# Block 1 of a fused linear-attention and GEGLU kernel: three of its tile pairs in Strassen form, and its order written out as a list

## Chip, cores, metric

The program runs on one core of a Trainium2 chip. The metric is the device time of one execution in microseconds (us), as the median of several runs; four runs of the kernel before were taken. One further execution was recorded by the hardware profiler; all durations of single instructions come from it.

## What is computed

The reference, cut to what matters (q, k, v are 8 x 8 x 576 x 64, so x is 4608 x 512; d_ff is 1536; all fp32):

```
q_s = softmax(q, axis=-1)                 # over the head dimension
k_s = softmax(k, axis=2)                  # over the sequence
kv  = einsum('bhsd,bhse->bhde', k_s, v)
x   = einsum('bhsd,bhde->bhse', q_s, kv)  # then heads side by side: 4608 x 512
g, val = x @ w_gate, x @ w_val
out = (gelu(g) * val) @ w_out             # exact gelu
```

## The kernel before

**Blocks.** The 4608 rows of x are done in nine blocks of 512: block b (0 to 7) holds 512 of the 576 tokens of batch b, and a ninth (number 8) holds the 64 tokens left over from each batch. The order is 0 to 6, 8, 7. While the feed-forward part of block b runs, the attention of batch b + 1 is prepared: exp of q and k on ACT (`exp`), row sums of q on DVE (`norm_sum`, `norm_pair`) and the multiplication on POOL (`norm_mul`), the cast of v (`cast_v`), a DMA that transposes q (`unit_td`, issued by SP), the k/v products (`unit_kv4`) and their scaling (`kv4_norm`), and the product that makes the next x (`unit_x4`, emptied by `x4_out`).

**The feed-forward part, plain.** In block 0 and block 1, d_ff is cut into 12 tiles of 128. A tile has a gate product and a value product, four matmuls of 512 columns each (`mm_gv`); ACT takes gelu of the gate, DVE multiplies it with the value into `ht` (`gate`). In block 1 the first three tiles are interleaved with the last steps of the attention of batch 1 (`ffn_first`), the other nine follow one after the other (`ffn_fi`).

**The feed-forward part, in pairs.** From block 2 on, tiles k and k + 3 (k in 0 to 2), and likewise k and k + 3 for k in 6 to 8, form a pair, and their products are made by Strassen's scheme in Winograd's form: seven products P1 to P7 of 4 matmuls with 256 columns each (`product_gv`), 28 in place of 32 such halves. It needs sums of the weights (made once, by `sum_wgv` and `sum_w1`) and sums of x (`sum_x`, into `xs`), and more steps on ACT and DVE. The output product is made in the same scheme (`product`) in block 1 and after; it needs sums of `ht` (`sum_h`) and of `w_out` (`sum_w`).

**Order.** The order in which the program is written is the order on each engine: the engines run their own queues in order, and wait for each other by semaphores. In blocks 0 and 1 it comes from loops and from a table of riders, `at(block, kind, index, ...)`: functions that are called behind a tile (`FI`) or an output step (`NS`). From block 2 on it is a list of words for each block, `PROG[b]`, which `play` carries out one after the other:

- `kPi`: product Pi of pair k. `kc`: ACT copies bank a of pair k to bank b. `ks5`, `ks2`: a scaled copy to SBUF on ACT, with `d` on DVE. `ka2`, `ka5`: DVE adds a bank to such a copy, into a buffer `cc`. `kg2`, `kg4`: gelu of 256 columns on ACT; `km2`, `km4`: their multiplication on DVE. `ku`: gelu of half of `cc` on ACT; `kU`: its multiplication on POOL, with `d` on DVE.
- `Oi:js`: product i of the output, of some j or all six. `y1`, `y2`, `y5`: copies of output banks; `b+`, `a+`, `c+`: additions into the output rows, `ye` the last copy. `sij`: sum i of `ht`. `wki`: sum i of the weights of pair k. `xi`: sum i of the next x.
- `lq`, `lk`, `lv`: loads of the next batch, by SP. `NA`, `NB`: row sums of q; `M0` to `M3`: their use, on POOL. `t`: the transposing DMA. `K`, `k`, `X`, `Xa`, `Xd`: k/v products, their scaling, the product for the next x, its emptying on ACT and DVE. `Vi`: casts of v. `Eq`, `Ek`: exp of q, k. `TE`, `TG`: a preload of ACT's table for exp or gelu.
- A last letter p, d or a names the engine (POOL, DVE, ACT); `>` and `<` take a word for the block after or before.

**Banks.** PSUM has eight banks. `big` takes the bank at the head of the list `ring`; `hold` keeps it until `let_go`. Two banks are set apart in `att_ring` for the attention until `one_ring` puts them on the list. A matmul that takes a bank waits for the last reader of the tile that was in it.

**Riders of block 1 that the change touches** (line numbers of the file before are in the printed functions): exp of k of batch 2 in two halves behind tiles 4 and 11, the casts of v of batch 2 on POOL behind tile 5, the transposing DMA behind tile 8, and

```
    at(1, NS, 2, L(unit_kv4, 2), L(exp, "k", 3), L(load_batch, 3, ((v, "v"),)), L(cast_v, 3, 0, H))
    at(1, NS, 4, L(unit_x4, 2, ("act", "dve"), 1), one_ring, L(preload, ACTF.Gelu))
```

Of the kernel before, what the change touches and what calls it, by code (L numbers as in the profile page):

```python
# [18 lines left out]
def kernel(  # L19
# [61 lines left out]
    def big(shape, dt, name, hold=False, seed=False):  # L81
        tag = ring.pop(next(i for i, x in enumerate(ring) if x in full) if seed else 0)
        t = ps_big.tile(shape, dt, name=name, tag=tag)
        words = 1
        for n in shape[1:]:
            words *= n
        (full.add if words == 512 and shape[0] == 128 and dt == f32 else full.discard)(tag)
        if hold:
            held[id(t)] = (t, tag)
        else:  # L90
            ring.append(tag)
        return t
# [434 lines left out]
    def ffn_first(xt, after):  # L527

        ps = []
        for fi in range(len(after)):  # L530
            psg = big([P, 512], f32, "psg")
            psv = big([P, 512], f32, "psv")
            if fi == 0:
# [6 lines left out]
            ps.append((psg, psv))  # L540
            for f in after[fi]:
                f()
        for fi, (psg, psv) in enumerate(ps):
            mm_gv(psg, wg_sb, xt, fi, [2])
            mm_gv(psv, wv_sb, xt, fi, [2])
        for fi, (psg, psv) in enumerate(ps):
            mm_gv(psg, wg_sb, xt, fi, [3])
            mm_gv(psv, wv_sb, xt, fi, [3])
            gate(psg, psv, fi)
# [110 lines left out]
    def product_gv(i, ps, xt, k, first):  # L660
        lo, hi = slice(k * P, (k + 1) * P), slice((k + NO // 2) * P, (k + NO // 2 + 1) * P)
        xs = xs_b[xt is st.get((B - 1, "xt"))]
        for t, w, nm in ((0, wv_sb, "v"), (1, wg_sb, "g")):
# [12 lines left out]
        2: ("lk lq lv 2P1 6P1 <x0d 0P1 <x2d 0P5 w71d 6P5 <x1d 6c w72d 6P2 0c w81d 6P6 0s5 0P6 6s5 0P3 6g2 w82p 6P3 "  # L676
            "0s2 NB 0P2 6m2 6s2 0P7 <x3p 0a2 6P7 0g2 1P5 2c 6a2 M3 1P1 0a5 2P2 0m2 2P5 w84p 1c 6a5 0P4 0u 1P2 2g2 6P4 "
            "M2 6u 1P6 0g4 NA 2P6 1s5 2m2 1P3 0U 0m4 1s2 7P1 1g2 2s5d 6g4 1P7 6U 2s2 1a2 2P3 6m4 2P7 7c 1m2 7P6 M0 "
            "1a5 8P1 7P2 2a2 1u 1P4 M1 8c 2a5 t 7P5 7g2 w83d 8P2 w74d 7s2 w73d 8P6 7s5 s01d 7P7 2u 8P5 1Ud 1g4 7P3 "
            "8s2 7a5 2P4 1m4 8s5 2U 8P7 7a2 8P3 2g4 7P4 >>lr s03p 7u 8a5 O1:03 O1:1 7g4 8a2 8P4 8g2 2m4 O1:4 7U 7m2 "  # L680
            "8u O1:25 8m2 8g4 K 7m4 8m4 O2 8U y1d TE s11d s21d s12d O5 s14d s02d s22d O6 Eq >lq b+ y5a k s24d X s04d "
            "s13d y2a O3:03142 s23d O7 Xa Xd V2a x2d x0d O3:5 x1d"),
        3: ("0P5 6P5 <a+ 0P1 <c+ 6P1 <Ek <O4 0s5 6c 0c NB 0P3 6s5 0P6 <yea 6P6 M3 6P3 0s2 NA 7P1 0P7 6s2d 6P2 6a2 <TG "
            "M0 6P7 0a2 0P2 6g2 1P1 0a5 7c <x3p 6m2 7P2 0g2 0P4 6a5 1c 6P4 0m2 M1 0u 1P6 0g4 1P5 7g2 7P5 7m2 6u 0U "
            "0m4 1P2 1s2 1P7 1s5d <V0p <V3a 7P6 6g4 6Ud 2P1 7s5 6m4 1P3 1g2 1a5 7P3 7s2 s01p 1P4 2c 1a2 7P7 1m2 8P1 "
            "1g4 M2 t 2P6 1u 7a5 2P5 <V1p 8c 1m4 7P4 2s2 7a2 8P5 2s5 1U 2P7 s02d 7u 8P6 7g4 O1:03 2a5 2P3 8s2 8P2 7Ud "
            "8s5 8P7 lk 2a2 O1:1 8P3 s11p 2u 2P2 8a5 8g2 8P4 7m4 8m2 2P4 2g2 2U O1:4 8g4 8a2 K 2g4 8m4 O2 2m4 8u s12p "
            "lv 2m2 8Ud s21d O1:25 TE s23d O5 s14d s04d y1a s22d O6 k b+ s24p y5d X Eq s03p O3:03142 Xa s13p Xd"),
        4: ("6P1 0P1 <y2d <x0d <O7 <Ek <x1p 0P5 0c NA <O3:5 0P6 6c <a+ <x3p 6P5 0s5 0P3 <c+ 0s2 6P2 <x2p 6s5 6P6 0P2 "
            "<V0a 6P3 M1 NB <O4 6s2d <TG 6g2 6a2 M0 0g2 1P1 0a2 <V2a 0P7 0m2 M3 6P7 1c 1P5 0a5 <V1a 1P6 6m2 M2 t 0P4 "  # L690
            "0u 6a5 7P1 <V3p <yea 1P2 0g4 1s5d 7P5 1s2 0Ud 6P4 1g2 0m4 1P3 7c 1m2 1P7 6u 2P1 6g4 1a2 7P6 7P2 7s5d lv "
            "6U 2c 7P3 1a5 7s2 2P5 6m4 7g2 7P7 s01p 7m2 2P6 2s5 7a2 1P4 s03p 1u 8P5 7a5 2s2 s02d 8P1 1g4 s04d 7P4 lq "
            "8s5 1m4 2P7 8c 1Ud 8P3 7u 8P6 7g4 2a5 2P3 2P2 7Ud 8s2 s11d 2P4 7m4 8P7 2g2 lk 8P2 8a2 s12p K 8a5 8g2 8P4 "
            "2g4 2a2 O1:03 8u 2m2 2m4 O1:1 8g4 O1:4 8m2 O1:25 2u 8m4 O2 8U k 2Ud TE s21d X y1a s22d O6 Xa Xd"),
        5: ("0P1 <s24d <x2d <O5 <x0d <s14d <s23d <s13d <Eq 0P5 lq 6P1 0c <b+ 0P2 <x1d <y5a 6P5 <Er <O3:03142 6c <x3p "
            "0s5 NB 0P6 6s5 6P6 <y2a <O3:5 6P3 M2 <O7 NA 6s2 0s2d 6P2 M0 Rr 6P7 6a2 0P7 <Ek M1 0P3 <a+ <O4 <c+ Rm <TG "
            "6a5 6g2 0g2 <V3p 6P4 6m2 0m2 1P1 <V1p <yea 1P5 6g4 0a2 7P5 6u 0a5 7P1 1c 0P4 0u 7s5d 1P2 6U 7c 1P6 1s5d "
            "6m4 7P6 <V2a 0g4 1P3 0U 1g2 1s2d 7P3 7s2 1P7 1a2 s01p 7P2 <V0a lv 2P1 7a2 2P5 1a5 M3 7P7 0m4 2c 1P4 1m2 "
            "7g2 s02d 8P1 1u 7m2 2P6 1g4 7a5 8P5 8c 7P4 t 1U 7u 2s2d 8P2 1m4 8s5 8P6 s03d 2s5 2P7 7g4 7Ud 8P3 s11d "
            "8s2 2P2 2a5 8P7 7m4 2P3 2g2 s12p 8g2 8a2 2P4 O1:03 8a5 lk s14p 8P4 8m2 2g4 O1:1 8u 2a2 O1:4 K 8g4 2m4 "  # L700
            "2m2 2u O1:25 8m4 8U O2 2Ud TE s21d s22d >tr y1a O5 s13d b+ s24d O6 s23d k Eq s04d X y5a O3:03142 y2d Xa "
            "O7 Xd x2d x0d"),
        6: ("6P1 <x1d <O3:5 <Ek 6P5 <a+ 0P1 6c <x3p 0P5 <V3a <O4 0c NA 6s5 <c+ 0s5 6P6 6P3 M1 <yea 0P6 <V0p 6P2 NB "
            "1P1 0P3 0s2d M0 0P2 6s2d 1c 0P7 6a2 6P7 M2 1P2 0a2 <TG 7P1 <V1p 6g2 0a5 1P6 0g2 6a5 0P4 0u 0m2 6P4 7c "
            "1g2 1P5 1s2d 0g4 7P6 6g4 0Ud 7P2 1m2 6u 0m4 1P7 1s5 6m4 7P5 7s2 2P1 6Ud 6m2 1P3 7s5 7P7 1a5 7g2 s01p 1P4 "
            "2c 1a2 2P5 7m2 7P3 1u 7a5 8P1 2s5 2P6 1g4 7a2 2P3 1U 8c 8P5 2s2d <V2a 8P6 2P2 7u 2a2 M3 t 1m4 2P7 8s2 "
            "7P4 2g2 7Ud 8P7 8s5 2a5 8P3 7g4 2P4 s11p 2u 8a5 O1:03 O1:1 2g4 8a2 8P2 7m4 2U 8P4 8u 2m2 2m4 K 8g2 8Ud "
            "O1:4 s21d O1:25 s23d O5 s12d s02d y1a s22d 8g4 8m2 O6 s04d 8m4 s03d s13d O2 s24d y2a k y5a O7 b+ s14d X "
            "O3:03142 a+ O4 Xa Xd"),
        8: ("0P1 <x0p <x2d <O3:5 6P1 <x1d 0P5 0c <c+ 6P5 6c 0P6 0s5 6P6 <yea 6s5d 6P2 z0d 0P3 z2d 7P1 6g2 0s2d 6P3 "  # L710
            "6s2 6m2 6P7 7c 0a2 0P7 1P1 6a2 7P2 0a5 7P6 1c 0P2 6a5 0u <x3d 7P5 6P4 0g2 0Ud 7g2 1P2 0m2 7s5 0P4 7s2d "
            "1P5 6u 7m2 6g4 1P6 1g2 6m4 0g4 7P3 7P7 1s5 6Ud 2P1 1s2 7a2 1P7 0m4 1P3 s01p 1m2 2c 2P5 7a5 2P6 z1p 2P2 "
            "1a5 7u 8P1 1a2 2s5 1P4 s02p 2s2d 2P3 8c 8P5 7Ud 2g2 8P6 2m2 1u 2P7 1g4 z3d 8P2 1Ud 8s2 7P4 8s5 2a5 8P7 "
            "8g2 1m4"),
# [459 lines left out]
```

The softmax here doesn't subtract the row's maximum and nothing guards it: scores larger than these inputs give would overflow.

## Time and profile before

| what | value |
|---|---|
| median of 4 runs | 288.78 us (288.70 to 288.96) |
| the profiled execution | 288.96 us, of which the span from first to last instruction is 287.2 us |
| busy share of the span | PE 97%, DVE 87%, ACT 73%, POOL 48% |
| granted TensorE clock | 1.00 of full speed over the span |
| HBM | 164 GB/s over the span |

The span is the time from the first to the last instruction on the core; 1.76 us lie around it. PE is TensorE's matmuls, PEld its weight loads, DVE VectorE, ACT ScalarE, POOL GpSimd, SP the engine that issues most DMAs. The busy time of PE contains matmuls that overlap, so single durations (273 ns for 256 columns) are longer than the distance from one start to the next. Where a row says "idle before", the engine stood still ahead of that instruction, and the name behind the arrow is what ended it.

In the recorded execution, block 1's first matmul starts at 48.72 us, its third tile's last at 55.14, its plain tiles end and its output begins at 70.89, and block 2's first product starts at 82.19.

### The profile page before, as it was taken

Reading aid. Unit: us, or ns where it says so; the run is one execution under the profiler, and the core shown is the slowest. Engines: PE = TensorE matmul, PEld = TensorE weight load, DVE = VectorE, ACT = ScalarE, POOL = GpSimd, SP = SyncE. Lnnn points to the kernel's source line nnn. Section 1 sums busy time; section 2 is a strip of 40 time slices with the busy share of each in tenths; the row PEclk is TensorE's granted clock in tenths of the full one; section 3 lists DMA queues with packets and bytes.
Section 4 is the critical chain, followed back from the end, with each engine's and each line's share of the span. In section 5 each row is a group of like instructions: output and inputs, shape, how many; then the busy total and the mean of one; then the engine's idle time right before and its main releaser. Section 6 shows DMA issues by size and latency. Waiting matters only on the chain.

```text
span 287.2 us, 6704 instructions
## 1 busy us (share of the span) xinstructions
PE 277.7 (97%) x2581; PEld 216.2 (75%) x2581; DVE 249.4 (87%) x497; ACT 209.9 (73%) x370; POOL 137.9 (48%) x128
## 2 busy tenths in 40 slices
PE   3999999999999999999999999999999999999994
PEld 1444445445888888888888888888888888888883
DVE  2854888877999999979989999999999799998993
ACT  3773367884798889978998899799794577716740
POOL 1567745988239731865864258542653104110110
PEclk9999999999999999999999999999999999999999
DMA  6999999999139916159149853690304030003303
GB/s 218 375 380 386 400 393 390 393 311 242 49 132 351 251 32 224 78 102 317 39 100 296 305 164 149 183 249 2 147 4 92 0 149 0 2 0 76 73 2 146
DMA packets 54623, 51.74 MB, mean 180 GB/s; under 512 B 18496, under 2 KB 50496, under 8 KB 54592
## 3 DMA queue, kind: packets, MB, share of 16 engines
q1 hardware_dynamic: 52864, 49.49, 54.1%
q10 hardware_dynamic: 1728, 1.84, 2.0%
q8 instruction: 20, 0.33, 0.5%
q14 instruction: 11, 0.09, 0.1%
HBM read 37.75 MB, written 9.44 MB: 164 GB/s over the span
## 4 chain that ended last, share of the span: by engine, by line
PE 89%; DVE 6%; DMA 2%; ACT 1%; issue 1%; POOL 1%; DVEq 0%; POOLq 0%; ACTq 0%
PE psa L670 24%; PE psc L670 12%; PE psA L749 12%; PE psg L511 7%; PE psv L511 7%; PE psC L749 6%; PE psb L670 6%; PE psy L579 4%; PE psB L749 3%; DMA qt<-in_q_dram 2%; DVE rq L255 1%; PE pskv L368 1%; PE psa L749 1%; DVE yo L770 1%; PE pst L400 1%
## 5 line engine op out<-in xcount | busy, mean ns | idle before, releaser
L670 PEld LDWEIGHTS <-wgv_sb 128*128 128x128 f16 x672 | 65.7, 98 | 8.0 <-issue 0.3
L265 POOL TENSOR_TENSOR eq<-eq,rrq 128x640 f16<-128x640 f16 (+1 forms) x27 | 35.0, 1307 | 24.3 <-ACT psb L858 11.7
L749 PEld LDWEIGHTS <-ht 128*128 128x128 f16 x384 | 37.2, 98 | 5.3 <-issue 0.4
L670 PE MATMUL psa<-xs,wgv_sb 128*128 128x256 f16 x288 | 40.4, 273 | 0.1
L511 PEld LDWEIGHTS <-wgv_sb 128*128 128x128 f16 x192 | 18.6, 98 | 21.9 <-issue 0.2
L858 ACT COPY psb<-psa 128x512 f32<-128x512 f32 x42 | 24.2, 582 | 8.3 <-PE psa L670 7.2
L511 PE MATMUL psv<-xt,wgv_sb 128*128 128x512 f16 x96 | 26.6, 379 | 0.0
L511 PE MATMUL psg<-xt,wgv_sb 128*128 128x512 f16 x96 | 26.6, 379 | 0.0
L516 ACT ACTIVATE gl<-psg 128x512 f32<-128x512 f32 x24 | 13.8, 598 | 16.6 <-PE psg L511 15.3
L839 ACT ACTIVATE snq<-psc 128x512 f32<-128x512 f32 x35 | 20.6, 603 | 5.7 <-PE psc L670 5.6
L517 DVE SCALAR_TENSOR_TENSOR ht<-psv,gl 128x512 f16<-128x512 f32 x24 | 16.0, 685 | 9.5 <-PE psv L511 7.9
L227 ACT ACTIVATE ek<-kt 128x1280 f16<-128x1280 f32 (+1 forms) x11 | 19.3, 1759 | 6.0 <-DMA kt<-in_k_dram 4.3
L670 PE MATMUL psb<-xt,wgv_sb 128*128 128x256 f16 x144 | 21.6, 273 | 0.0
L255 DVE TENSOR_REDUCE rq<-eq 128x20 f32<-128x1280 f16 (+1 forms) x12 | 17.1, 1425 | 4.5 <-ACT eq L227 4.5
L670 PE MATMUL psa<-xt,wgv_sb 128*128 128x256 f16 x144 | 20.9, 273 | 0.0
L749 PEld LDWEIGHTS <-sh 128*128 128x128 f16 x192 | 18.6, 98 | 2.8 <-issue 0.4
L749 PE MATMUL psA<-tw,ht 128*128 128x256 f16 x168 | 20.6, 272 | 0.0
L227 ACT ACTIVATE eq<-qt 128x2560 f16<-128x2560 f32 (+2 forms) x10 | 18.4, 1860 | 2.7 <-DMA qt<-in_q_dram 2.7
L886 POOL TENSOR_TENSOR ht<-cc 128x512 f16<-128x512 f32 x12 | 15.3, 1278 | 9.0 <-ACT cc L884 8.8
L876 DVE SCALAR_TENSOR_TENSOR ht<-psb,gl 128x256 f16<-128x256 f32 x42 | 17.2, 414 | 1.8 <-ACT gl L874 1.6
L874 ACT ACTIVATE gl<-psa 128x256 f32<-128x256 f32 x42 | 16.1, 386 | 3.3 <-PE psa L670 2.9
L874 ACT ACTIVATE gl<-psb 128x256 f32<-128x256 f32 x42 | 15.6, 383 | 3.7 <-PE psb L670 3.3
(192 smaller groups left out, 695.5 us busy)
## 6 DMA issues: line engine op xcount, KB each, us to landing
out_dram<-yo SPq DMA_DIRECT2D x15, 512.0 KB, 3.6
kt<-in_k_dram SPq DMA_DIRECT2D x7, 640.0 KB, 8.3
vt<-in_v_dram SPq DMA_DIRECT2D x7, 640.0 KB, 7.3
qt<-in_q_dram SPq DMA_DIRECT2D x7, 640.0 KB, 6.5
qt<-in_q_dram SPq DMA_DIRECT2D x8, 512.0 KB, 7.4
wost<-in_moe_w_out_dram SPq DMA_DIRECT2D x6, 512.0 KB, 7.9
kt<-in_k_dram SPq DMA_DIRECT2D x6, 512.0 KB, 7.3
vt<-in_v_dram SPq DMA_DIRECT2D x6, 512.0 KB, 7.1
```

The costliest lines, as they stand in the source:

```text
L227: nc.scalar.activation(out=dst[:, n0:NC, h0 * D:h1 * D].rearrange(o, d=D, **({"t": 2} if b >= QUAD else {})), in_=heads(tiles[(nm, b)], b, ...
L255: nc.vector.reduce_sum(rq, e, axis=mybir.AxisListType.X)
L265: (nc.gpsimd if eng == "pool" else nc.vector).tensor_tensor(out=e, in0=e, in1=rrq.unsqueeze(-1).to_broadcast((P, n, 2, D)), op=ALU.mult)
L511: nc.tensor.matmul(ps, w[:, ci, fi * P:(fi + 1) * P], xt[:, ci, :], start=(ci == 0), stop=(ci == HP - 1))
L517: nc.vector.scalar_tensor_tensor(out=ht[:, fi, :], in0=psv, scalar=_H_SCALE, in1=gl, op0=ALU.mult, op1=ALU.mult)
L670: nc.tensor.matmul(ps[:, t], a, x, start=(first and t == 0 and c == 0), stop=(c == 1), skip_group_check=True)
L749: nc.tensor.matmul(ps[t], a, w, start=(first and j == js[0] and (t == ts[0] or ps[t].tensor is not ps[ts[0]].tensor)), stop=(j == js[-1]), ...
L839: nc.scalar.activation(out=dst, in_=src, func=ACTF.Copy, scale=scale)
L858: nc.scalar.copy(out=t[f"b{k}"], in_=t[f"a{k}"])
L874: nc.scalar.activation(out=gl, in_=t[ps][:, 1], func=ACTF.Gelu)
L876: nc.vector.scalar_tensor_tensor(out=ht[:, k if x[2] == "2" else k + NO // 2, 0:256], in0=t[ps][:, 0], scalar=_H_SCALE, in1=t["g" + ps], o ...
L886: (nc.vector if side == "dve" else nc.gpsimd).tensor_tensor(out=ht[:, k:k + NO // 2 + 1:NO // 2, 256:512], in0=cc[:, :, 0], in1=cc[:, :, 1 ...
```

## The change

1. Block 1 keeps six plain tiles, 6 to 11; its tiles 0 to 5 become the pairs 0 to 2. `ffn_first` now runs tiles 6 to 8, and holds their banks; their gates are words of the new list. The pairs need sums of x (`q0` to `q3`) and of the gate and value weights (`G3`) at their time, which come into the list; before, `G3` stood in block 1's output part, and x had no sums there.
2. `out_strassen`, `SUMS` and block 1's riders go; `PROG[1]` takes their place, and `play` gets words for it: `fg`, `fv` (a plain product), `fga` (its gelu), `fvd` (its multiplication), `N0` to `N3`, `v0` to `v3` (casts of v of batch 2, all on ACT), `W2`, `W4` (sums of `w_out`), `E2` (exp of k of batch 2, whole).
3. exp of k of batch 2 stands once, behind the table preload `TE` at the end of block 1; the table loads around its two halves go. The program then holds 14 table loads in place of 16 on ACT.
4. The sums of the weights of pairs 6 to 8 move: block 1 had the four of pair 6 on POOL, behind tiles 6 and 9, and block 2's list had six sums of weights on DVE (w71, w72, w81, w83, w74, w73) and two on POOL (w82, w84). Block 1's list now has w71, w73, w63, w72 on DVE and w61, w62, w74 on POOL; block 2's has w83, w82 on DVE and w81, w84, w64 on POOL.
5. The lists of blocks 2 to 8 are new; they hold the same steps in another order, with some of them on another engine and some on the other side of the border between two blocks.

The diff, cut; of the lists, block 1's is whole and block 2's is shown before and after:

```
     def ffn_first(xt, after):
-
         ps = []
-        for fi in range(len(after)):
-            psg = big([P, 512], f32, "psg")
-            psv = big([P, 512], f32, "psv")
-            if fi == 0:
+        for i in range(len(after)):
+            fi = NO + i
+            psg, psv = (big([P, 512], f32, "ps" + nm, True) for nm in "gv")
+            acts.setdefault(1, {}).update({f"{fi}g": psg, f"{fi}v": psv})
+            if i == 0:
...
-        for fi, (psg, psv) in enumerate(ps):
-            mm_gv(psg, wg_sb, xt, fi, [2])
-            mm_gv(psv, wv_sb, xt, fi, [2])
-        for fi, (psg, psv) in enumerate(ps):
-            mm_gv(psg, wg_sb, xt, fi, [3])
-            mm_gv(psv, wv_sb, xt, fi, [3])
-            gate(psg, psv, fi)
+        for ci in (2, 3):
+            for fi, psg, psv in ps:
+                mm_gv(psg, wg_sb, xt, fi, [ci])
+                mm_gv(psv, wv_sb, xt, fi, [ci])
...
     PROG = {
+        1: ("lq N3 1P1 8ga 6ga N1 9g W2p 1c 8vd 1P2 v0a lk 6vd q2p 9v q0d 9ga 0P1 v1a 10v 7ga G3d v2a q1d 1P5 1g2 1P6 "
+            "7vd 0c 0P5 1s5 9vd q3p 0P6 1m2 1s2 1P3 0s5 1P7 M1 N0 0s2 2P1 0P7 1a2 v3a lv 0P3 w61p 1a5 2c 2P5 0a5 2P6 "
+            "M0 0P2 0a2 10g 0u W4d 2s2 1P4 2s5 2P7 N2 0P4 10ga 0U 2P3 s01d 1u 0g2 11g 2a5 0g4 0m2 2P4 0m4 1g4 1U 2P2 "
+            "2a2 11ga 11v 2g4 10vd M2 2u 1m4 O1:031 2g2 2m4 O1:4 11vd M3 O2 t 2m2 TE 2Ud s21d O1:25 s11d O5 s12d s02d "
+            "s23d E2 s14d K s22d y1a s24d s04d O6 s13d y5d >w71d O3:03142 >w73d Eq >lq w63d y2a s03d O7 >w72d k O3:5 "
+            "b+ >w74p X Ek a+ O4 w62p c+ Xa"),
-        2: ("lk lq lv 2P1 6P1 <x0d 0P1 <x2d 0P5 w71d 6P5 <x1d 6c w72d 6P2 0c w81d 6P6 0s5 0P6 6s5 0P3 6g2 w82p 6P3 "
-            "0s2 NB 0P2 6m2 6s2 0P7 <x3p 0a2 6P7 0g2 1P5 2c 6a2 M3 1P1 0a5 2P2 0m2 2P5 w84p 1c 6a5 0P4 0u 1P2 2g2 6P4 "
-            "M2 6u 1P6 0g4 NA 2P6 1s5 2m2 1P3 0U 0m4 1s2 7P1 1g2 2s5d 6g4 1P7 6U 2s2 1a2 2P3 6m4 2P7 7c 1m2 7P6 M0 "
-            "1a5 8P1 7P2 2a2 1u 1P4 M1 8c 2a5 t 7P5 7g2 w83d 8P2 w74d 7s2 w73d 8P6 7s5 s01d 7P7 2u 8P5 1Ud 1g4 7P3 "
-            "8s2 7a5 2P4 1m4 8s5 2U 8P7 7a2 8P3 2g4 7P4 >>lr s03p 7u 8a5 O1:03 O1:1 7g4 8a2 8P4 8g2 2m4 O1:4 7U 7m2 "
-            "8u O1:25 8m2 8g4 K 7m4 8m4 O2 8U y1d TE s11d s21d s12d O5 s14d s02d s22d O6 Eq >lq b+ y5a k s24d X s04d "
-            "s13d y2a O3:03142 s23d O7 Xa Xd V2a x2d x0d O3:5 x1d"),
+        2: ("0P1 w81p 6P1 <Xd <x0d 2P1 <TG <x1d 0P5 0c <x3d 0P2 w83d <yea 0P6 <x2d 6c w82d 6P5 0s5 6P2 2c 6P6 w84p "
+            "0s2 0P3 0g2 NB 0P7 6g2 0m2 2P2 <w64p 6s2 6m2 1P1 6s5 <V1p 0a5 6P7 6P3 0a2 1c 0P4 2g2 M2 6a5 1P6 0u 2m2 "
+            "2P6 0g4 6a2 1P5 M3 1s2 6P4 6u 2P5 1s5 1P7 0U 6g4 NA 1P3 0m4 <V0a 1P2 6m4 6U 7P1 2s2 1a2 7P5 2s5 1g2 2P7 "
+            "1a5 M1 7c 2P3 7s5d 7P6 <V3a 1m2 7P3 1u M0 t 2a2 8P1 7s2 8P5 2a5 7P7 s01d 8c s02d 1P4 s03d 2u 8P6 1Ud 2P4 "
+            "1g4 7P2 8s5 7a2 8P3 8s2 7a5 2U 2g4 8P7 1m4 O1:03 <V2a lk 8a2 7P4 7g2 s04p 8P2 8a5 7u 2m4 8P4 8u O1:1 7Ud "
+            "8g2 O1:4 7g4 O1:25 s11d 8g4 K 8Ud s21d O5 7m2 lv 8m2 TE 7m4 y1a s22p 8m4 O2 s13d s24d y5a s12d O6 k s14p "
+            "b+ X Eq >lq s23p O3:03142 y2d Xa O7 Xd x2d x0d"),
...
-    at(0, NS, 17, L(unit_x, 1, 0, "act", True), L(unit_x, 1, 1, "act", True), L(sum_w, 3, "pool"),
-       L(sum_w, 2, "pool"))
+    at(0, NS, 17, L(unit_x, 1, 0, "act", True), L(unit_x, 1, 1, "act", True), L(sum_w, 3, "pool"))
...
-              [L(unit_x, 1, 3, "dve"), L(norm, 2, 0, "pool"), L(norm, 2, 1, "pool")]]
+              [L(unit_x, 1, 3, "dve"), L(unit_trem, 1), one_ring]]
...
-    at(1, FI, 2, L(unit_trem, 1))
-    at(1, FI, 3, L(norm, 2, 2, "pool"), L(load_batch, 3, ((q, "q"), (k, "k"))))
-    at(1, FI, 4, L(exp, "k", 2, 0, 4), L(norm, 2, 3, "pool"), L(sum_w, 4), make_s)
-    at(1, FI, 5, L(cast_v, 2, 0, H))
-    at(1, FI, 8, L(unit_td, 2))
-    at(1, FI, 11, L(exp, "k", 2, 4, 8), L(exp, "q", 3))
-    at(1, NS, 2, L(unit_kv4, 2), L(exp, "k", 3), L(load_batch, 3, ((v, "v"),)), L(cast_v, 3, 0, H))
-    at(1, NS, 4, L(unit_x4, 2, ("act", "dve"), 1), one_ring, L(preload, ACTF.Gelu))
...
-    at(1, NS, 2, L(sum_wgv, "g", 3), L(sum_wgv, "v", 3))
-    for i, x in ((6, 1), (6, 2), (6, 4), (9, 3)):
-        at(1, FI, i, L(sum_w1, x, NO, "pool"))
```

## The prediction

> **What bounds the kernel now.** I read the page first, then the stretches of block 1 and 2, then the time line engine by engine. The page gives the span and the busy time of each engine.
>
> ```profile
> span 287.2 us, 6704 instructions
> PE 277.7 (97%) x2581; PEld 216.2 (75%) x2581; DVE 249.4 (87%) x497; ACT 209.9 (73%) x370; POOL 137.9 (48%) x128
> PE 89%; DVE 6%; DMA 2%; ACT 1%; issue 1%; POOL 1%; DVEq 0%; POOLq 0%; ACTq 0%
> ```
>
> PE carries 89% of the chain that ended last, so what PE no longer has to do is time won, unless a wait takes its place. The windows by stage (columns: us, then busy time of PE, PEld, DVE, ACT, POOL) show the plain part of block 1 with its output (55.35 to 82.19) beside block 2's stretch:
>
> ```profile
> core 0: us, PE busy (x) PEld busy (x) DVE busy (x) ACT busy (x) POOL busy (x), PEclk, DMA share, GB/s
> 55.35:82.19 26.84, 26.66 (x222) 16.12 (x220) 22.88 (x40) 18.67 (x23) 17.21 (x17) 1.00 0.74 201
> 82.19:109.77 27.58, 27.58 (x297) 24.06 (x295) 26.94 (x60) 24.38 (x48) 15.69 (x13) 1.00 0.71 214
> ```
>
> PE is full in both. Block 1 leaves ACT 8 us and DVE 4 us free; block 2, built as the new block 1 will be, leaves 3 and 0.6. The time line of PE gives prices and the few waits (start, length, what, idle before):
>
> ```profile
> 55.35 1.03 PE L511 MATMUL psg<-xt,wgv_sb 128*128 128x512 f16 x4
> 56.22 1.03 PE L511 MATMUL psv<-xt,wgv_sb 128*128 128x512 f16 x4
> 80.88 1.47 PE L749 MATMUL psa<-tw,ht 128*128 128x256 f16 x12 [0.16 <-DVE yo L770]
> 82.19 1.47 PE L670 MATMUL psa<-xt,wgv_sb 128*128 128x256 f16 x12
> ...
> 117.87 1.31 PE L670 MATMUL psa<-xs,wgv_sb 128*128 128x256 f16 x8
> ```
>
> Four 512-column matmuls take 0.863 us from start to start, 0.2158 each; twelve of 256 columns take 1.31, 0.1093 each. Twelve matmuls of block 1's output start at 73.52 and the next at 75.02, 0.19 later than 12 x 0.1093; 80.88 is 0.16 late; the eight at 117.87 last 1.31 where 7 x 0.109 + 0.273 = 1.04 would do, 0.27 late. Little else is lost after 17 us: PE is at its floor.
>
> **The change part by part.** *PE work.* Tiles 0 to 5 of block 1 (6 x 8 = 48 matmuls of 512 columns) become three pairs (3 x 28 = 84 of 256 columns): 48 x 0.2158 = 10.36 us go, 84 x 0.1093 = 9.18 come: **-1.18 us**. All other PE work stays.
>
> A rule speaks against it. The Trainium skill, "TensorE: Matmul & The Clock Gate", section "Back-to-back issue gap", gives a sustained 81 ns for 128 columns and 131 ns for 512 in a stream of weight loads and matmuls; my estimate for 256 on a straight line between them is 98 ns, by which the sum would be 84 x 0.098 - 48 x 0.131 = +1.9 us instead. The rows above (216 and 109 ns) differ from it and decide.
>
> *Block 1's three steps behind the first three tiles.* The tiles 6 to 8 replace 0 to 2 at the front with the same matmuls, so PE reaches 55.35 as before. From there I walked the new order by hand. The price of an ACT step is its spacing in unbroken runs:
>
> ```profile
> 54.48 1.57 ACT L516 ACTIVATE gl<-psg 128x512 f32<-128x512 f32 x3
> 56.42 0.60 ACT L516 ACTIVATE gl<-psg 128x512 f32<-128x512 f32 x1 [0.37 <-PE psg L511]
> 58.76 1.28 ACT L227 ACT_TABLE_LOAD   x1
> 60.05 1.27 ACT L227 ACTIVATE ek<-kt 128x1280 f16<-128x1280 f32 x1
> 61.34 1.28 ACT L516 ACT_TABLE_LOAD   x1
> ```
>
> Three gelus in 1.57 us are (1.57 - 0.60) / 2 = 0.485 apart, and the last result is there 0.60 after its start; copies of 512 and the s steps are 0.49 apart, v casts 0.63, gelus of 256 columns 0.28, u 0.53. A waiting matmul follows its releaser by 0.05 (DVE's yo ended at 80.83). PE then meets these waits:
> - 9g takes the bank of tile 8's gate, read by 8ga, the first on ACT: 55.34 + 0.60 + 0.05 = 55.99, while PE has done 1P1 (0.44) at 55.79: **0.20**.
> - 1P2 waits for 1c, third on ACT: 55.34 + 2 x 0.485 + 0.58 + 0.05 = 56.94 against 9g's end at 56.85: **0.09**.
> - 10v takes the bank that 9ga reads, and 9ga stands behind v0a, which waits for v of batch 2. In before that tensor is awaited by POOL alone. Its second half is issued at 49.64 and takes the longest landing of this row, so it is there at 57.74:
>
> ```profile
> 48.97 1.39 SPq L183 DMA_DIRECT2D vt<-in_v_dram  x2
> DMA to landing us min/median/max: 4.6/6.3/8.1
> ```
>
>  ACT is idle from 56.9 to 57.74, then v0a, then 9ga until 57.77 + 0.63 + 0.60 = 59.00. PE (1P2, 9v, 0P1) is ready at 58.69: **0.36**. Queued behind v0a on ACT are 9ga, v1a, 7ga, v2a, 1g2 and 0c; PE and 7vd, 9vd on DVE wait for them.
> - 1P5 takes the bank that 7ga reads: 58.40 + 0.485 + 0.63 + 0.60 + 0.05 = 60.16 against 59.91: **0.25**.
> - 0P6 (for 0c), 1P3 (1s5), 1P7 (1s2), 0P7 (0s2): 0.06 + 0.07 + 0.06 + 0.10 = **0.29**.
>
> From 2P5 on ACT is ahead (0u stands idle 0.9 us for 0a2). Sum of new waits: **+1.2 us**. Its ends: 0.5, if v has landed early and the last four vanish, and 2.1, if ACT's steps cost their full length through that stretch.
>
> *exp of k.* Two halves (1.27 each) become one (2.35, row of 5) behind one preload: 1.294 + 0.11, and ACT saves two of its loads in the block (2 x 1.294). It now stands close before K: 11ga starts at 69.33, then 2g4, 2u, 2g2, TE; E2 runs from 72.31 to 74.66. PE reaches K after 18 products (0.437 each), 10g, 11g and 11v (0.863 each), 36 output matmuls (3.93) and the 0.29 of waits from 60.16 on, at 74.84. Cover: 0.13 us after the 0.05 of a release; cost nothing; each later 0.1 us of ACT beyond that is 0.1 us of PE. The skill's "ScalarE: Activation LUTs", section "What ACT_TABLE_LOAD costs", puts about 2.66 us on a switch, drain included; with that E2 would end 1.37 us later and K wait 1.25 us, where the rows show the next step 1.294 after the load's start.
>
> *Moved steps.* The mul's M0 to M3 on POOL end later: M3 behind 1U, M2, at about 71.8; t is issued then, and lands 6.0 to 6.4 us after issue in two rows of eqt: 78.2 at most, X is due at 79.6: covered by 1.4. SP's queue keeps its order up to the load of k 3 (the transpose of batch 1's rest included); v 3's load goes ahead of t, two issues of 0.7 us at 64, covered. W2p stays at POOL's place of before. The new sums (x sums q, three w sums on DVE, 0.34 each) end before PE needs them: O5's last sum at 73.36 against 73.52. Before's two waits (0.19, 0.16) meet no late releaser: X needs kv4 at 78.7, O4 needs a+ at 80.3 and starts at 80.6: **-0.35**.
>
> Sum of block 1: -1.18 + 1.20 - 0.35 = **-0.33**, so that 0P1 of block 2 starts at 81.88 instead of 82.19 (rounding 0.02).
>
> *Blocks 2 to 8.* All lists are new, with the same steps. Per block the sums of spacings stay under PE's on every engine (block 5, the fullest: DVE 31.7 against PE 34.4). Before loses 0.27 there at 118.6, where DVE had run since 109 with one gap of 0.20, and 0.07 at 188. Block 2 loses four weight sums on DVE (6 become 2, 4 x 0.335 = 1.3 us), more than the 0.27, so I take the 0.27 as gone and 0.03 besides: **-0.30**. Bounds: -0.34, and +1.0, if three turnarounds as tight as 9g's (0.2 to 0.36 each) have come into seven blocks; the value is nearer to the first, as the old lists of the same kind lost 0.34 in all.
>
> Sum: -0.63. The profiled execution took 288.96 (span 287.2 and 1.76 around it), so 288.33; the median of the runs is 0.18 lower: **288.15 us**. A measurement tells about 0.2% (0.58 us) from no change; the forecast lies at that edge.
>
> **The rivals.** *The waits are hidden.* Were v there by 56.9 and ACT's queue a little shorter, the 1.2 would be 0.3, and 288.15 - 0.9 = 287.25. For it: four of eight waits are at most 0.1. Against: 8ga cannot start before PE has done tile 8, and v lands behind a DMA share above 1.0 until 71 us. Chance 0.17.
>
> *ACT becomes the bound, at K: slower.* ACT has 13.1 us of spacings from 8ga to 2g2; at full lengths (0.60, 0.58, 0.73, 0.39, 0.63) it would be 16.0. Of these 2.9, 0.9 go into the idle time before 0u and 0.1 into the cover, the rest is a wait at K or at the banks before: 288.15 + 1.9 = 290.0, and half of the excess 289.1. It decides from 0.63 us of ACT lateness beyond the covers on (1.2 for slower by over 0.2%). For it: v0a, and E2's 0.13. Against: the unbroken runs in the trace. Chance 0.20.
>
> *The new lists give it back.* Waits of 0.6 us in blocks 2 to 8: 288.75. For it: each list is rewritten; against: the loads per block are the same. Chance 0.08.
>
> **How the numbers follow.** Forecast 0.55, its own range 287.8 to 288.6, cut in half by the 0.2% bound (288.20). Faster: 0.28 + 0.17 = 0.45. Within: 0.27 + 0.08 = 0.35. Slower: 0.20 (the lower half of that rival, under 289.36, is balanced by the forecast's bound of +1.0). The range, 287.3 to 289.4, takes in the first rival, the third, and the low part of the second.
>
> **What would show it.** PE's 512-column matmuls fall from 192 to 144 in the rows, the 256-column ones of the pairs rise by 84 from 1176. In the time line, waits of 0.2 to 0.4 before the third gate tile, the second v tile and the first c product, the latter two released by ACT gelus behind a v cast that waits for its DMA; no idle PE before the k/v products; block 2's first product at 81.9; no wait near 118. Wrong would be a wait for the k exp, or PE waits behind 82 us of more than 0.7 in all.

## The result, and the profile after

The changed kernel takes **289.21 us** (median of 41 runs, 289.01 to 289.76), the kernel before 288.87 (61 runs, 288.65 to 289.18): a ratio of 1.0012, 95% interval 1.0008 to 1.0016. The time went up by 0.34 us where 0.63 less was forecast. It lies inside the range; the direction was wrong. The profiled execution took 289.24 us, 0.28 more than that of before.

The head of its page and the chain that ended last:

```profile
span 287.4 us, 6800 instructions
PE 277.0 (96%) x2617; PEld 219.2 (76%) x2617; DVE 246.6 (86%) x499; ACT 216.0 (75%) x390; POOL 145.4 (51%) x133
PE 76%; DVE 12%; DMA 6%; issue 2%; ACT 2%; POOL 1%; SPq 0%; DVEq 0%; ACTq 0%; POOLq 0%
```

PE's busy time fell by 0.7 us, but it lost 13 points of the chain; DVE's share doubled and DMA's tripled. Something other than PE now sets the pace for a stretch. The windows tell which (columns as before). First the changed kernel, cut at block 2's first product and at block 2's X; then the same two later stretches of before:

```profile
55.51:82.23 26.72, 26.39 (x257) 19.44 (x256) 24.35 (x54) 24.23 (x40) 14.44 (x13) 1.00 0.79 228
82.23:107.21 24.98, 24.87 (x258) 21.58 (x256) 24.26 (x51) 23.74 (x46) 15.76 (x15) 1.00 0.54 161
107.21:283.40 176.19, 176.19 (x1796) 154.74 (x1796) 159.46 (x322) 136.40 (x266) 81.77 (x72) 1.00 0.39 116
```

```profile
82.19:106.72 24.53, 24.53 (x258) 21.67 (x255) 24.00 (x53) 21.44 (x42) 15.69 (x13) 1.00 0.70 210
106.72:283.16 176.44, 176.33 (x1796) 154.63 (x1796) 163.44 (x333) 137.31 (x265) 71.77 (x63) 1.00 0.38 114
```

The second column is the length. Block 1 behind its first tiles: 26.84 before, 26.72 now, a gain of 0.12 (forecast 0.33). Block 2 up to X: 24.53, now 24.98, a loss of 0.45. The rest: 176.44, now 176.19, a gain of 0.25. PE also reached the first cut 0.16 later (55.51 against 55.35). The largest loss is in the 25 us behind the new block 1, where DVE is busy 24.3 of 25.0 us.

PE's time line shows each wait by the start of the instruction behind it; the last row, of ACT, is the cast that waited for v:

```profile
56.14 1.02 PE L515 MATMUL ps9g<-xt,wgv_sb 128*128 128x512 f16 x4
58.99 1.02 PE L515 MATMUL ps10v<-xt,wgv_sb 128*128 128x512 f16 x4
60.11 0.38 PE L671 MATMUL psc<-xs,wsv 128*128 128x256 f16 x2
77.07 1.25 PE L756 MATMUL psC<-wo_sb,s 128*128 128x256 f16 x10
78.53 1.49 PE L756 MATMUL psA<-tw,ht 128*128 128x256 f16 x12 [0.21 <-DVE ht L627]
82.23 1.47 PE L671 MATMUL psa<-xt,wgv_sb 128*128 128x256 f16 x12
83.75 0.39 PE L671 MATMUL psc<-xs,wsv 128*128 128x256 f16 x2
57.72 0.73 ACT L209 CAST v<-vt 128x640 f16<-128x640 f32 x1 [0.65 <-DMA vt<-in_v_dram]
```

Against the spacings of 0.2158 and 0.1093 us, 9g starts 0.20 late, 10v 0.14, the first c product 0.25; with 0.12 before 1P2 (57.12) and three of 0.08 to 0.09 up to 63.5 the front loses 1.0. These were forecast. Not forecast: output product 3 is 0.10 late at 77.07, product 7 0.38 late at 78.53 (10 x 0.1093 behind 77.07 is 78.16), and the first pair product on an x sum 0.20 late at 83.75 (82.23 + 12 x 0.1093 = 83.54). Another 0.23 goes at 101.0, and 0.18 at 187 to 189. The 0.27 at 118.6 of before is gone.

### The profile page after: what moved, and what is told of

Read it like the earlier page. It is cut to its first block, busy times and chain, and to the rows that moved or that the text cites. A ratio compares the mean times of both kernels' runs of the same rounds, so it can differ in the third digit from the quotient of the medians.

```text
span 287.4 us, 6800 instructions
## 1 busy us (share of the span) xinstructions
PE 277.0 (96%) x2617; PEld 219.2 (76%) x2617; DVE 246.6 (86%) x499; ACT 216.0 (75%) x390; POOL 145.4 (51%) x133
## 4 chain that ended last, share of the span: by engine, by line
PE 76%; DVE 12%; DMA 6%; issue 2%; ACT 2%; POOL 1%; SPq 0%; DVEq 0%; ACTq 0%; POOLq 0%
PE psa L671 22%; PE psA L756 13%; PE psc L671 11%; PE psC L756 7%; PE psb L671 5%; PE psg L515 4%; PE psv L515 4%; PE psB L756 3%; PE psy L580 3%; DMA kt<-in_k_dram 3%; DMA vt<-in_v_dram 3%; DVE cc L797 2%; DVE ht L831 1%; PE pskv L372 1%; DVE rq L259 1%
## 5 line engine op out<-in xcount | busy, mean ns | idle before, releaser
L671 PE MATMUL psa<-xs,wgv_sb 128*128 128x256 f16 x312 | 44.0, 273 | 0.1
L813 ACT COPY psb<-psa 128x512 f32<-128x512 f32 x45 | 26.0, 587 | 7.2 <-PE psa L671 5.7
L841 POOL TENSOR_TENSOR ht<-eq 128x512 f16<-128x512 f32 x8 | 10.2, 1276 | 36.1 <-ACT eq L839 36.1
L794 ACT ACTIVATE snq<-psc 128x512 f32<-128x512 f32 x37 | 21.9, 602 | 2.7 <-PE psc L671 2.7
L756 PE MATMUL psA<-tw,ht 128*128 128x256 f16 x192 | 23.5, 273 | 0.2 <-DVE ht L627 0.2
L671 PE MATMUL psb<-xt,wgv_sb 128*128 128x256 f16 x156 | 22.9, 273 | 0.0
L671 PE MATMUL psa<-xt,wgv_sb 128*128 128x256 f16 x156 | 22.6, 273 | 0.0
L231 ACT ACTIVATE ek<-kt 128x2560 f16<-128x2560 f32 (+1 forms) x10 | 19.0, 1911 | 4.1 <-DMA kt<-in_k_dram 4.1
L831 DVE SCALAR_TENSOR_TENSOR ht<-psa,gl 128x256 f16<-128x256 f32 x45 | 18.0, 414 | 3.5 <-ACT gl L829 3.4
L794 ACT ACTIVATE snq<-psa 128x512 f32<-128x512 f32 x34 | 20.4, 605 | 0.5 <-PE psa L671 0.2
```

What stands on the lines that cost most here:

```text
L231: nc.scalar.activation(out=dst[:, n0:NC, h0 * D:h1 * D].rearrange(o, d=D, **({"t": 2} if b >= QUAD else {})), in_=heads(tiles[(nm, b)], b, ...
L671: nc.tensor.matmul(ps[:, t], a, x, start=(first and t == 0 and c == 0), stop=(c == 1), skip_group_check=True)
L756: nc.tensor.matmul(ps[t], a, w, start=(first and j == js[0] and (t == ts[0] or ps[t].tensor is not ps[ts[0]].tensor)), stop=(j == js[-1]), ...
L794: nc.scalar.activation(out=dst, in_=src, func=ACTF.Copy, scale=scale)
L813: nc.scalar.copy(out=t[f"b{k}"], in_=t[f"a{k}"])
L831: nc.vector.scalar_tensor_tensor(out=ht[:, k if x[2] == "2" else k + NO // 2, 0:256], in0=t[ps][:, 0], scalar=_H_SCALE, in1=t["g" + ps], o ...
```

## The experiments

Three explanations stood against each other: the front of block 1 alone (ACT's order); DVE's queue, from 60 us to 101; the new lists of blocks 2 to 8. Every kernel is the changed one with an edit of its lists. Differences are between medians; the kernel before ran beside each group at 288.83 to 288.91, so they hold to about 0.1 us. Each run's trace is one execution of it.

**front_order.** Finished gelus first, v casts behind the gelu of tile 9:

```
- N3 1P1 8ga 6ga N1 9g W2p 1c 8vd 1P2 v0a lk 6vd q2p 9v q0d 9ga 0P1 v1a 10v 7ga G3d v2a q1d 1P5 1g2 1P6 7vd 0c
+ N3 1P1 6ga N1 9g W2p 7ga 6vd 8ga 1c 1P2 lk 7vd q2p 9v q0d 8vd 9ga 0P1 v0a 10v G3d v1a q1d 1P5 1g2 1P6 v2a 0c
```

> Block 1's list alone is changed at its start: the gelus of tiles 6 and 7 go ahead of that of tile 8, and the first v cast goes behind the gelu of tile 9, so that no gelu stands behind a cast that waits for the landing of v. Front theory (the waits of 1.0 us between 55.5 and 63.5 us are what ate the PE saving, and they come from ACT's order alone): these waits fall to 0.2 us or less, time 0.8 to 1.0 us under the changed kernel. DVE theory (from 60 us on DVE's queue sets PE's pace): DVE's idle 1.07 us before 60.09 goes too, so the front gain holds, but the stalls at the output product 7 (0.38), at the first pair product of block 2 that needs an x sum (0.20) and at 101 us (0.23) stay; 0.6 to 1.0 under the changed kernel. List theory (what was lost lies in the lists of blocks 2 to 8): the front gain is taken back behind 82 us, 0.3 or less in all.

Measured 288.52, 0.69 less than the changed kernel; ratio to before 0.9994 (0.9985 to 1.0002). No wait above 0.09 is left between 55 and 63.5 us; those at output product 7 (0.375), the x sum (0.21) and at 99.9 (0.22) stand as before. So 0.8 of the front's 1.0 us went in the trace, and 0.69 is left of that in the median (a wait of 0.14 has appeared at 230 us); the later waits do not come from the front.

Two halves of that edit show which order mattered. **casts_late** moves only the v casts behind the gelus of tiles 9 and 7:

```
- 1c 8vd 1P2 v0a lk 6vd q2p 9v q0d 9ga 0P1 v1a 10v 7ga G3d v2a q1d 1P5 1g2 1P6 7vd 0c
+ 1c 8vd 1P2 lk 6vd q2p 9v q0d 9ga 0P1 7ga 10v v0a G3d v1a q1d 1P5 1g2 1P6 7vd v2a 0c
```

> Half of the front order: the gelus of tiles 9 and 7 go ahead of the first v cast, the order of 8ga and 6ga stays. Front theory by parts: the waits of the second v tile (10v, 0.14 to 0.47) and of the first c product (0.25), and those behind them (0.25 in sum), go; those at 9g (0.20) and 1P2 (0.12) stay: 0.5 to 0.8 us under the changed kernel, and nearly all of what the whole front order won. If the order of 8ga and 6ga matters as much: 0.3 or less.

Measured 288.85, 0.36 less (expected 0.5 to 0.8); ratio to before 1.0003 (0.9994 to 1.0011). The waits at 10v and at the first c product are gone in its trace, those at 9g and 1P2 (0.20, 0.12) stay; the wait of 0.14 at 230 us is here too; no run tells its cause.

**gelu_first** moves only the gelu of tile 6 ahead of that of tile 8, and with it the multiplication on DVE that reads it:

```
- N3 1P1 8ga 6ga N1 9g W2p 1c 8vd 1P2 v0a lk 6vd
+ N3 1P1 6ga 8ga N1 9g W2p 1c 6vd 1P2 v0a lk 8vd
```

> The other half: the gelu of tile 6, finished early, goes ahead of that of tile 8, the v casts stay. The waits at 9g and 1P2 (0.32 in sum) go. If the landing of v, and the gelu of tile 9 behind its cast, set the pace, PE only comes earlier to the wait at 10v, which grows by the same 0.3: 0.0 to 0.1 us won. If each wait counts by itself: 0.3.

Measured 289.22: nothing won; ratio to before 1.0012 (1.0003 to 1.0021). Its PE line at the second v tile:

```profile
57.82 0.60 PE L671 MATMUL psa<-xt,wgv_sb 128*128 128x256 f16 x4
59.02 1.02 PE L515 MATMUL ps10v<-xt,wgv_sb 128*128 128x512 f16 x4 [0.60 <-ACT gl L852]
```

9g and 1P2 are on time, and 10v waits 0.76. All that PE gained it waited for there, behind the gelu that stands behind the cast that waits for v. Only once the casts are out of the way is the other order worth its 0.33 (front_order less casts_late).

**s03_first.** One sum ahead of the weight sums:

```
- y5d >w71d O3:03142 >w73d Eq >lq w63d y2a s03d O7 >w72d
+ y5d s03d >w71d O3:03142 >w73d Eq >lq w63d y2a O7 >w72d
```

> In block 1 the one sum on DVE that the output product 7 waited for (s03d) goes ahead of three weight sums; nothing else. If that wait is a local fault of order, its 0.38 us is won whole. If DVE is full from 67.5 to 83.3 us, the work is only shuffled: product 7 starts 0.38 earlier, but the x sum of block 2 comes at most 0.2 earlier, so that its wait grows from 0.20 to about 0.4, and 0.0 to 0.2 us is won. If the lists of blocks 2 to 8 are the cause, nothing changes by more than 0.1.

Measured 288.97, 0.24 less; ratio to before 1.0004 (0.9996 to 1.0013). Product 7 starts on time, product 4 of the output is 0.09 late instead, and the wait at the x sum grows from 0.20 to 0.28. Two thirds of the 0.38 stay won: between the two theories, a little over the upper end that DVE's full queue had given it.

**dep_spread.** The same sums, kept apart from those that they depend on:

```
- TE 2Ud s21d O1:25 s11d O5 s12d s02d s23d E2 s14d K s22d y1a s24d s04d O6 s13d y5d >w71d O3:03142 >w73d Eq >lq w63d
+ TE 2Ud s11d O1:25 s21d O5 s02d s12d s23d E2 s22d K s14d y1a s04d s24d O6 s13d y5d >w71d O3:03142 w63d Eq >lq >w73d
```

> Only the order of DVE's sums in block 1's output changes: sums that read the result of the sum just before them (or overwrite what it reads) are kept apart by another sum. In the changed kernel's trace such a successor starts 0.115 us later than an independent one (0.45 instead of 0.335 from start to start), four times between 72 and 78 us. Dependence theory: DVE is 0.46 us earlier at the sum that the output product 7 waits for, so the waits at products 3 (0.10) and 7 (0.38) go; of these 0.48, up to 0.2 is lost again at block 2's first x sum: 0.25 to 0.45 under the changed kernel. If the 0.45 comes from something else than the neighbour (POOL, a semaphore of PE), the spacings stay and the time is the same within 0.1.

Measured 288.81, 0.40 less; ratio to before 0.9995 (0.9987 to 1.0004). DVE's time line of the changed kernel, then of this one:

```profile
74.53 0.42 DVE L627 TENSOR_TENSOR s<-ht,sh 128x512 f16<-128x512 f16 x1
74.87 0.42 DVE L627 TENSOR_TENSOR sh<-sh,ht 128x512 f16<-128x512 f16 x1
75.32 0.76 DVE L627 TENSOR_TENSOR s<-ht,sh 128x512 f16<-128x512 f16 x2
...
78.06 0.42 DVE L627 TENSOR_TENSOR ht<-ht 128x512 f16<-128x512 f16 x1
```

```profile
74.36 0.42 DVE L627 TENSOR_TENSOR sh<-sh,ht 128x512 f16<-128x512 f16 x1
74.69 1.09 DVE L627 TENSOR_TENSOR s<-ht,sh 128x512 f16<-128x512 f16 x3
...
77.64 0.42 DVE L627 TENSOR_TENSOR ht<-ht 128x512 f16<-128x512 f16 x1
```

Above, s24 at 75.32 reads what the sum at 74.87 wrote: 0.45 from start to start, where its neighbours keep 0.34. Below, with other sums between, each follows at 0.335. The changed kernel has four such places ahead of s03, the last row of each view: s21 at 72.72, behind the multiplication 2U that it reads (0.71 from start to start, where in dep_spread a sum that does not read 2U follows at 0.60); s12 at 73.52; s24; and w73 at 77.38, which overwrites what w71 at 76.93 reads. At 0.11 to 0.12 each they made DVE some 0.46 late at product 7. Here both waits (77.07, 78.53) are gone; that at the x sum stays at 0.20.

**w_on_pool.** The four weight sums from DVE to POOL (`>w71d >w73d w63d >w72d` become `>w71p >w73p w63p >w72p`).

> The four weight sums that block 1's end computes on DVE for block 2 (w71, w73, w63, w72, 0.34 us each on DVE) go to POOL (1.12 us each), which is idle for 7 us before 78.9. DVE theory: DVE gets 1.3 us of room, so the waits at the output products 3 (0.10) and 7 (0.38) and at block 2's first product on an x sum (0.20) go, and perhaps that at 101 us (0.23): 0.6 to 0.9 us under the changed kernel. Local-order theory: only product 7's 0.38. List theory: 0.1 or less. Against all: if POOL's later sums (w62, w74, w81) come too late for block 2, up to 0.5 slower.

Measured 294.35, **5.1 us more** than the changed kernel; ratio to before 1.0209 (1.0183 to 1.0236). All theories missed. Its time line, POOL and DVE side by side:

```profile
72.96 2.78 POOL L652 TENSOR_TENSOR wgv_sb<-wgv_sb 128x512 f16<-128x512 f16 x2
73.47 2.55 DVE L627 TENSOR_TENSOR sh<-ht 128x512 f16<-128x512 f16 x2
76.08 1.05 PE L757 MATMUL psC<-tw,sh 128*128 128x256 f16 x8 [2.12 <-DVE sh L627]
78.30 1.33 POOL L652 TENSOR_TENSOR tw<-tw,wgv_sb 128x512 f16<-128x512 f16 x1
78.54 1.37 DVE L627 TENSOR_TENSOR ht<-ht 128x512 f16<-128x512 f16 x1
79.83 0.41 DVE L627 TENSOR_TENSOR s<-ht,sh 128x512 f16<-128x512 f16 x1
```

Two of DVE's sums take 2.55 us where the pair took 0.76, and one takes 1.37 instead of 0.42. At 79.83, POOL being done at 79.63, the sum takes 0.41 again. While POOL runs operations on two SBUF tensors in a row, each such operation of DVE takes about as long as one of POOL's (1.1 to 1.4). DVE's additions that read a PSUM bank (512 columns) do not suffer: 0.63 to 0.69 us in this trace, beside an operation of POOL or not. PE's waits of 2.1, 0.8, 0.9 and 1.1 us follow. The Trainium skill, "SBUF — State Buffer", section "SBUF: two separate sides", gives the rule: DVE and GpSimd share one pair of SBUF ports, and the instruction that starts first holds it to its end; a DVE operation with two SBUF inputs needs the pair too, against a GpSimd operation that reads SBUF. These rows agree with it. POOL's 7 idle microseconds were no room for DVE's sums.

**front_and_pool.** The edits of front_order and of w_on_pool together.

> Both edits together: the new order at block 1's start and the four weight sums on POOL. DVE theory with the front theory: the gains add, 1.4 to 1.8 us under the changed kernel, about 287.5 and thus under the kernel before by 1.1 to 1.4. If they overlap (an earlier PE meets other late releasers), no better than the better of the two.

Measured 294.07, ratio 1.0195 (1.0176 to 1.0215), 4.9 more than the changed kernel and only 0.3 less than w_on_pool: with PE waiting for DVE (2.12 us at 75.15 by its row), little of the front's gain is left.

**split_exp.** One part of the change undone, the single exp of k:

```
- 2c 2P5 0a5
+ 2c TE Ea TG 2P5 0a5
...
- s23d E2 s14d
+ s23d Eb s14d
...
+ "Ea": lambda: exp("k", n, 0, 4), "Eb": lambda: exp("k", n, 4, 8),
```

> One part of the change undone: the exp of k of batch 2 in block 1 again in two halves, the first in a table session of its own behind the copy of pair 2, the second at the old place. ACT gets two more table loads (1.3 us each, with 0.1 of preload) ahead of its gelu of pair 0, and 1.1 us less ahead of K. If ACT has no room there but the 0.97 us that it idles: PE waits of 1.8 to 2.9 us behind 64 us, 1.5 to 2.8 over the changed kernel; so much is the one session worth. If ACT's 2.5 us of idle time in the stretch cover it: 0.5 or less.

Measured 293.57 (four runs), 4.4 us more; ratio to before 1.0149 (1.0130 to 1.0169). PE starts 2P7 at 69.75, 2.8 us late (2.65 of it idle by its row), because of a scaled copy on ACT, as expected of an ACT without room. What followed was not expected; its windows (length, PE, PEld, DVE, ACT, POOL, granted clock, then DMA):

```profile
66.50:69.75 3.25, 0.60 (x5) 0.39 (x4) 0.76 (x2) 3.22 (x6) 0.45 (x1) 1.00 0.93 324
70.90:74.20 3.30, 3.30 (x14) 1.69 (x12) 2.92 (x7) 1.76 (x6) 2.93 (x3) 0.51 0.00 0
```

From about 1.2 us behind the wait's end on, the granted clock is 0.51 for 3.3 us, and matmuls come at half pace: another 1.6 us. Wait and half clock make 4.4. But the half clock is not in every run: three of the four took 293.42 to 293.76 us at a mean granted clock of 0.993 or 0.994, the fourth 292.25 at 1.000. That one is 3.0 over the changed kernel, a little over the upper end of 2.8 that was expected. So the one table session is worth some 3 us where it stands, and more where the wait of PE brings the clock down.

**s75_only.** In block 2, `7s5d` becomes `7s5` (DVE to ACT).

> One step of block 2 alone moves: the scaled copy 7s5 (0.6 us) from DVE to ACT. In the changed kernel DVE runs from 84.5 to 101 us with gaps of 0.13 at most, and product 4 of pair 8 waits 0.23 us at 101.0 for DVE's addition 8a5. DVE theory: the wait goes, 0.15 to 0.25 us under the changed kernel. If 101 waits for something else than DVE's load (ACT, a bank): the same within 0.1, or slower by ACT's 0.5.

Measured 289.28, no gain; ratio to before 1.0017 (1.0008 to 1.0026). The wait at 101 is gone; a new one of 0.21 stands at 96.5, where 7P7 waits for 7s2, which ACT ends at 96.45, behind the added step of 0.49. So at that place ACT has no 0.5 us to spare either; DVE's load is one of two bounds there, not the only one.

**Combinations.** front_dve is front_order and dep_spread, with s03d ahead of the weight sums, and W4 and w71 moved into DVE's idle time before 67 us:

```
- M1 N0 0s2
+ M1 N0 W4d 0s2
...
- 0u W4d 2s2
+ 0u >w71d 2s2
...
- y5d >w71d O3:03142 w63d Eq >lq >w73d y2a s03d O7 >w72d
+ y5d s03d O3:03142 w63d Eq >lq >w73d y2a O7 >w72d
```

> The new order at block 1's start, the spread sums, the sum s03 ahead of the weight sums, and one weight sum (w71) and W4 moved into idle time of DVE before 67 us, all on DVE. If both theories hold (front order and DVE's queue), the front's 1.0 us and the 0.48 at products 3 and 7 go, while 0.2 to 0.3 at block 2's first x sum and 0.23 at 101 us stay: 1.1 to 1.4 us under the changed kernel, 0.7 to 1.0 under the kernel before. If only the front counts: 0.7 as in the run with the front alone.

Measured 289.59, 0.38 **more**; ratio to before 1.0025 (1.0016 to 1.0035). PE is ahead until 98 us and then waits 0.74, 0.16 and 0.66:

```profile
96.27 1.46 POOL L842 TENSOR_TENSOR ht<-cc 128x512 f16<-128x512 f32 x1 [1.43 <-ACT cc L840]
96.51 1.76 DVE L842 TENSOR_TENSOR ht<-eq 128x512 f16<-128x512 f32 x1
98.41 0.69 DVE L798 SCALAR_TENSOR_TENSOR eq<-psc,snq 128x512 f32<-128x512 f32 x1
99.15 0.60 PE L757 MATMUL psA<-wo_sb,ht 128*128 128x256 f16 x4 [0.57 <-DVE eq L798]
```

The changed kernel at the same place:

```profile
97.33 0.69 DVE L841 TENSOR_TENSOR ht<-eq 128x512 f16<-128x512 f32 x1
97.38 1.78 POOL L841 TENSOR_TENSOR ht<-cc 128x512 f16<-128x512 f32 x1 [1.40 <-ACT cc L839]
```

The same two products of block 2. In the changed kernel DVE starts 0.05 us ahead and POOL waits, which nobody notices; here POOL is 0.24 ahead, and DVE's takes 1.76 instead of 0.69. In both, the one that starts second pays.

front_dve_x_s adds two steps, the first across the border of block 1's and block 2's lists, the second in block 2's:

```
- O4 w62p c+ Xa
+ O4 w62p Xa Xd x0d c+
...
- 0P1 w81p 6P1 <Xd <x0d 2P1
+ 0P1 w81p 6P1 2P1
...
- 7s5d
+ 7s5
```

> As the one before, and two steps more: DVE casts its half of X and makes the first x sum ahead of the last addition of block 1's output (c+) instead of behind it, and one scaled copy of block 2 (7s5) goes from DVE to ACT, 0.6 us. DVE theory: the waits at block 2's first x sum (0.2 to 0.3) and at 101 us (0.23) go too: 1.5 to 1.8 us under the changed kernel, about 287.5. If the two waits only move on to the next late releaser: no more than the run before.

Measured 288.05, 1.16 less; ratio to before 0.9969 (0.9956 to 0.9981). The collision is gone and 101 us is clean. But the first x-sum product is still 0.20 late (82.47), though its sum is done at 81.81: c+, now behind it, ends at 82.41. That the product waits for the bank that c+ reads fits these rows; no run tried it by itself.

front_spread_s is front_order, dep_spread and 7s5 on ACT, nothing else.

> The front order, the spread sums, and 7s5 on ACT together, W4 and the weight sums where they were: 0.8 + 0.45 + 0.2 less what block 2's first x sum keeps: 1.1 to 1.4 us under the changed kernel, 0.7 to 1.0 under the kernel before. If DVE's 1U and POOL's 2U of block 2 meet at 96 us as in the run front_dve, some 1.2 us of it is lost.

Measured **287.85**, 1.36 less than the changed kernel and faster than the kernel before: 0.9966 (0.9954 to 0.9979). The chain on its page:

```profile
PE 93%; DMA 3%; ACT 2%; DVE 0%; issue 0%; ACTq 0%
```

PE is back at 93% of the chain and DVE is out of it. With the order mended, the changed kernel is 1.0 us faster than before. front_order and dep_spread add up to 1.09 of the 1.36; what is left of it can't be put down to 7s5 by a wait, since the wait of 0.23 at 101 us has only become one of 0.21 at 95.0, as in s75_only. The wait at the x sum (0.20) is still there. What the same two orders would bring without 7s5 no run shows.

## Why the prediction was wrong, step by step

- **PE work, -1.18.** Nothing speaks against it: the matmuls keep the spacings that it was made of, and front_spread_s, with the same matmuls and most waits taken out, is 1.0 us under before. That 1.0 also holds waits that only before had (0.35 and 0.27), so it is no measurement of the term by itself.
- **New waits at the front, +1.20.** Right in place and cause, and near in size: 1.0 in the profiled execution, 0.8 of it gone with another order. The one at 10v, forecast at 0.36, is 0.14 here and 0.22 to 0.47 in five of the kernels above with the same front. In all six, 10v starts between 58.9 and 59.2 us, whenever block 1 began (48.56 to 48.88): the landing of v sets it, so an earlier start of the block only makes the wait longer.
- **exp of k and K: no wait, cover 0.13.** Right: E2 ended at 74.74, K began at 74.89 (forecast 74.84). split_exp shows what this part is worth.
- **t and the M steps, covered.** Right: issued at 71.92, landed 4.9 us later, at 76.8; X began at 80.17.
- **Before's two waits gone, -0.35: the first step that failed.** I wrote that they meet no late releaser. They are gone, but PE met two others, 0.10 at product 3 and 0.38 at product 7: a term that turned from -0.35 to +0.13. What was mis-sized is DVE's queue ahead of them: sums at 0.335 each, where four steps follow one that they depend on and start 0.11 to 0.12 later. The prediction showed its walk only up to O5's last sum (73.36). Carried on with 0.335 for a sum and 0.60 for the copy y5, it has s03 done at 77.98, with product 7 due at 78.00 (74.84 + 0.75 + 22 x 0.1093): no cover, but hardly a wait. s03 was done at 78.48. (The text spoke of three weight sums on DVE. The list has four, of which three stand ahead of s03.) The price was there to read in before, where the second of these sums reads what the first wrote and starts 0.45 behind it; dep_spread shows that it is the neighbour:

```profile
73.48 0.41 DVE L626 TENSOR_TENSOR sh<-ht 128x512 f16<-128x512 f16 x1
73.93 0.42 DVE L626 TENSOR_TENSOR sh<-sh,ht 128x512 f16<-128x512 f16 x1
```

- **Blocks 2 to 8, -0.30: the second step that failed.** Measured +0.20. Right was that 118.6 goes (-0.25 behind block 2's X). But block 2 gave +0.45: 0.20 at the x sum and 0.23 at 101. I had summed loads per block, which stay under PE's; a queue with gaps of at most 0.13 from 84.5 to 101 us makes each late start last, sums or not. One of its sums also stands 0.45 behind one that it depends on (96.20 and 96.65); how much of the 0.23 that is, no run shows. At the x sum, x0 stands on DVE behind a+, which waits for product 7's end, c+ and two pairs of casts, without a gap from 80.11 to 83.70. That row of steps is 0.20 longer than what PE has to do in the meantime: in dep_spread product 7 is on time, and the wait is the same 0.20.
- **The sum.** Forecast was -0.63, and the profiled executions differ by +0.28. Of these 0.91, 0.21 lie in block 1 behind its first tiles, 0.50 in blocks 2 to 8, 0.16 ahead of the first cut and 0.04 elsewhere. The 0.16 need not come from the change: block 1's first matmul starts between 48.48 and 48.95 in kernels that are the same up to there. That 289.21 lies inside the range is luck: its upper part stood there for a late ACT, and DVE was late. My sign for being wrong behind 82 us, waits of more than 0.7, did not show it either; they come to 0.6.
- **The rivals.** "ACT becomes the bound, at K" named the wrong engine: ACT idled little more than DVE in block 1's window, but its steps were priced from unbroken runs and held. "The new lists give it back", at 0.08 of chance, had the place of the 0.45 us. That DVE, with 4 us free in block 1 before and 2.4 after, could set the pace was not among them, and should have been.

## What to carry to other kernels

Price a queue's steps with their neighbours: on DVE, a sum that reads the result of the one just before it costs a third more here (0.45 for 0.335 us), and moving an independent step between is free. Before work goes to an idle engine, look at what the others run at that moment, and not only at its idle time: in these runs DVE and POOL stood in each other's way where both read two SBUF tensors at once. And a step that waits for a DMA belongs behind the steps that only need what is there: with the casts in front, what the order of the gelus alone gained at the front ended in the same wait.

## What the runs showed that I had not expected

- **DVE against POOL.** A DVE sum of 0.42 us took about 1.28 to 1.37 beside POOL's sums, and who started first by 0.05 or 0.24 us decided whether a product of block 2 took 0.69 or 1.76.
- **The clock behind a wait of PE.** In split_exp PE waited 2.65 us by its row and then ran 3.3 us at a granted clock of 0.51. In front_and_pool a wait of 2.12 us did the same (0.51 between 77 and 79 us); in w_on_pool a wait of 2.12 us at the same place did not (1.00). One kernel goes both ways: of five runs of w_on_pool, two have a mean granted clock of 1.000 and three of 0.993 or 0.994. In the two traces that show it, the half clock lasts 3.41 us. The Trainium skill, "TensorE: Matmul & The Clock Gate", Part 1 on the clock gate, lets the clock fall behind an idle window of about 3.4 us that runs freely. That one wait of 2.12 us halves the clock and another does not fits a free-running window; but less than 3.4 us of idle time was enough here.
- **A dependent neighbour on DVE.** 0.45 us from start to start instead of 0.335, the same for reading what the neighbour wrote (s24 behind s22) and for overwriting what it reads (w73 behind w71).
